# VectorE's exp with a shorter polynomial, 440 instead of 381 tiles on VectorE, and a new order of the steps

## The chip, the cores and the metric

The kernel runs on one core of a Trainium2 chip. The time is device microseconds of one execution, the median of three runs. A profile is one execution seen by the hardware profiler; its span is the time from its first to its last instruction.

## The reference

Four layers, one after the other, each of the form x + attention(layernorm(x)). The weights alternate: layers 1 and 3 use set A, layers 2 and 4 set B. x is 2048 x 512 in float32. There are 32 query heads of 16 dimensions, and one key head and one value head that all of them share.

```python
def _A_ref(x, wq, wk, wv, wo):
    ...
    q = (lambda x, *d: x.transpose(*d))((x @ wq).reshape(B, S, H, Dh), 0, 2, 1, 3)
    k = x @ wk
    v = x @ wv
    scores = jnp.einsum("bhqd,bkd->bhqk", q, k) * (Dh ** -0.5)
    p = _softmax(scores, axis=-1)
    o = jnp.einsum("bhqk,bkd->bhqd", p, v)
    return (lambda x, *d: x.transpose(*d))(o, 0, 2, 1, 3).reshape(B, S, H * Dh) @ wo
...
x = x + _A_ref(_layernorm(x, axis=-1), A_wq, A_wk, A_wv, A_wo)
x = x + _B_ref(_layernorm(x, axis=-1), B_wq, B_wk, B_wv, B_wo)
```

So per layer there are 32 x 2048 x 2048 exponentials, 537 million in all; they are most of the work outside the matmuls.

## The kernel before

**Tiles.** A layer's queries are cut into 4 blocks of 512 rows and 4 groups of 8 heads, and the keys into 32 pieces of 64; each such piece has two tiles of scores, 4096 over the four layers, each of 128 partitions x 1024 float32. The keys stand on the partitions, so the exponentials can be multiplied with V at once, and a column of ones in V gives the softmax's denominators.

**TensorE.** The array is used as eight small arrays of 64 rows x 32 columns: four on its upper 64 rows and four on its lower 64. The two halves of its rows are called row groups 0 and 1 here. A tile of scores (`st`, f16) is eight matmuls of 512 columns, four in each row group. The product with V (`acc`, float32) takes the upper 64 partitions of the exponentials in row group 0 (into `acc0`, letter E) and the lower 64 in row group 1 (into `acc1`, letter O). A float32 matmul stands twice in the trace, once for each of its two passes. E and O each treat 512 columns, either as two steps of 256 columns or, where the order gives E (or O) in two TensorE steps one after the other with nothing between, joined as one step of 512. All other matrix products (queries, keys and values, the output projection) go into one bank named `beside`, also cut into half steps, M or N, of one row group.

**The exponentials.** Most tiles go to ScalarE: `score()` makes the eight matmuls into one of two `st` buffers and one ACTIVATE (L777) into one of 16 buffers `pt`. The others go to VectorE. `score_v()` computes half a tile (letters V, W; 512 columns) into the single bank `by_v`. `exp_first()` (L809, letter I in the order) reads this half out of `by_v`, scales it and converts it to the integer whose bits are nearly the exponential's. When both halves are there, a chain of six instructions over 1024 columns follows (letters 0 and 1, since two chains can be under way): take the mantissa (L823), keep the exponent (L825), three steps of a polynomial in the mantissa (L826, L827, L828), and the product of both (L820).

**The order.** Everything above is written in an order fixed by hand in the string `ORDER`; the engines then run their own queues in that order and wait for each other by semaphores. S is a score for ScalarE; a to s are TensorE steps for the two row groups:

```python
STEPS = {"S": "SS", "a": "EO", "b": "NO", "c": "EN", "d": "MO", "e": "EM", "f": "VO", "g": "EV",
         "h": "WO", "i": "EW", "j": "VM", "k": "MV", "l": "E-", "m": "-O", "n": "N-", "o": "-N",
         "p": "M-", "q": "-M", "r": "V-", "s": "-V"}
```

A dash means that this row group gets nothing in the step. F and P are matmuls over the full 128 rows. X is one VectorE instruction of the layer's other work, G moves `acc` out (L925, L927), D a step of the division, Q a load of queries by a DMA on the SP queue. Y is `touch()` (L906): VectorE copies one column of `beside` into `seen`. It stands where the other row group is to go on in that bank, since the copy waits for TensorE's earlier work on it. All matmuls of the steps are issued in one function, `both()` (L495), row group 0 ahead of row group 1.

Of the kernel before, what the change touches and what calls it, by code (L numbers as in the profile page):

```python
# [49 lines left out]
LEAD = 1013283008.0  # L50
C0, C1, C2, C3 = 37.67991256713867, 23.053848266601562, 12.310662269592285, -0.15703019499778748
# [17 lines left out]
    "bSbISb0b0Sa0sSaaYISa0Sfc1Sc0qSaa1Sc0SccISa0qSaaXSa0SaaXSa0kSbIpSb0hSbIpS0a0Sa0aSiqISa0aSi1qSa0Saa1S0bSaY"
    "aISq0cSc0jSaaISc0SaaXSa0SaaXSr0mISQa0SF0SaaXSXaSPPPSPPGPSGsPISaXX0SaaS1a0Saa1Sa0SaaXSa0aSaXSaaXSa0SaPXSf"  # L70
    "aISl0SaaXSP0PSasXSaaISaXSa0aSXrPSaIaXSPSaaSXsXSaIa0SP0PPSa1Sa0rSaa1S0PPPSa1SPPP0SaaISa0SgaISPP0PSaXSa0aS"
    "hpISb0b0Sa0SgaISc0qSic1Sa0Saa1Sb0pSbpISaaY0SjcISc0qSQaaXSa0Shb1Sb0bSaISlGl0SpbGSb0mSaY0SicISc0qSfa1Sc0Sa"
    "aISc0c0SaSaXaSXXaDSaXXaDSaXXSaDXaXSa0sSaIaSXD0mSaaX1Sf0SaaISXaXSF00SaSaXaDSaXSgXmISaD0SflDSFD0SaaXS0SSIa"
    "XSaXaXD0SF0SXaS0aaSXsaISF0SaaXSa0SaaXSa0ShbIS0pa0SaDaS0kbSbIpSDb0rSalYDSc0SQaa1Sc0SaaISa0a0ScScGqqGSqq0S"
    "aaXSaXSaDXa0SaSaX0aSFXSsDaXISaXa0SXa0SaXX0fScIqSc0qScaDS0aSgaISDb0kSbbISbDpS0b0Sa0aSraISc0cSaXSa0aSaXaS0"
    "fScIcS0qc0Sa0sSaaISb0Shb1Sb0pSa1aS0aScIcS0eSaa0SsaISb0bSaXSa0aSaXrSaIa0Sc0Sc0cSm0SgaISb0pShb1Sa0SaaISQc0"
    "qq0ScSa0aSsaISbGpkGSpp0SaaXSa0SaaISaXSaDa0S0jcISc0qScc1Sj0aSa1Sa0aSb1pSaa0SbSbIbD0SkbSIaaY0SiSaXa0SaaISa"
    "XSaDa0SF0SaXa0SjcSIcq0Sic1Sm0Saa1Sb0pSbbISb0ShbISa0SaaY1Sa0Sic1SaXa0SaScIc0SqcSj0cSaaIS0aShb1S0bSaIaS0bb"
    "0SkbISa0SaaYS1Qgq0SeaXSa0SbaISlGpSl0bGSb0ShbISa0pSha1Sa0SaaY1Sc0SaaISc0cSc0SiaSIc0qSaaXSa0ShbISb0pSk0aIS"
    "a0aSa1Si0cScq1Sc0cSc1SaaY0SapSbIb0SaSaXaXXSrDaISaXXaSDaSXXgmDXSXa0SamXS1aXD0SamISa0SaXrSIaaXS0FSaXSa0aSa"  # L80
    "XrSXaDaS0FSXSDXSXXDSF0SISaXa0SaXsSQaIa0Sa0SF1SaXaS0aSaXaS0arSPGPPGSP0PSPPPISa0SaD0aSsaISa0aSaD1Sa0aSa1Sa"
    "0aSa0SfaISP0PSaaDSa0SaaD0SasSaIaDSa0Sg0aISPP0SaaXSaXSa0aSaX0SaaSXa0rSaaISXFS0faISXl0SaX0aSsXSIaaXX0SrSa1"
    "a0SaS1a0SaaIS0SgaISm0Sf1Sa0aSa1Sa0aSlISa0SsaISa0aSr1SQa0aS1Sa0aSGSGlISa0SgaISaD0Saa1Sa0SaaD1Sf0SaaIS0mSa"
    "0SgaISa0SgaDSm0SaaISDm0SaDaS0jcISc0Scc1Sj0qqSaaY1Sb0Sbb1Sbb0SbSaIaXSa0SicISc0Sic1Sa0qSaIaS0qa0SjaSIaq0Sa"
    "aS1a0ShbS1bp0SbbISb0SaaXSa0sSccISc0Sia1Sa0aScISa0a0SjcSaImY0SQhSa1a0Saa1SbGpSpGppS0pbSaIa0SbSaXaDS0scScI"
    "cS0cSi1cSD0aqSaIaY0Sa0ShbSIb0pSgbDSb0SbaXSaXXaDSaXXSaDaXXSa0SalISaXXSa0aXS0fISaX0aSa1Sa0rSaaXSXl0SFSXa0S"
    "aaISaXaSXa0Sa0Sas0SaaISF0SrSX0SISaXaSXaX0Sa0a0SasSaIa0SFS1aXSa0aSaXSa0aSF0SQaXa0SaSaXa0SajSGqqqGScIc0SaS"
    "a0mSkbISaDa0Sh0SaIa0SkaSIaaD0Skp1Sb0aSl1Sa0aScqISaDa0SjSaYIaSDn0SfaDS0lSa1aS0pSaaISaXsXSaISaXa0SXF0SaaXS"
    "0rSaaXS0aSaX0SaaISaX0SaXXs0SaIa0SSa1a0SrSa1a0SS1aaS0SISa0aSa0sSaaISa0SfaISl0Sa0a0SsSIaa0SQaS1ar0Saa1SGSG"
    "l0SaSaIa0SmSDa0aSsaISa0SaaD1Sr0SaaIS0sSaIa0SS1aaDSr0SaaD0SaSaDS0aaSI0Sa0aSsaISa0Saa1Sr0Saa1S0SaIaS0sSaIa"  # L90
    "S0rSa1aS0aSa1S0aaSIS0agSIm0Saa1Sa0SarS1aa0SSIaa0SsISa0aSr1Sa0aSa1Sa0SaaIS0sSaIaS0QrSa1aS0aSa1SGGSl0lSaIS"
    "a0mSaD0SamS0asSaIaD0SaSfaIS0ls0SaIaS0Sa1aSDa0SarSDa0aSDSa0aSppIpSb0b0SkbSIap0SpaS1ar0Saa1Sc0SccISc0qSiaI"
# [24 lines left out]
    "0a0gSmISa0eSrmXSaXa0SFSaX0SaaISaXS0agXSImXS0aaX0SaSaX0rSaaXXS0Sa1a0SSIa0Sa0SgaISa0Sar1Sa0aSm1Sa0aSISa0aS"
    "Qa0gSmISa0aSrGSGSl0aSaIS0amDS0a0SgaISa0SgaD1Sm0Saa1S0mSaaIS0SafDSaISDa0rSaaDS0cSc1cS0mqScIa0Sm0SgaISb0pS"
# [1239 lines left out]
```

## Time and profile before

| what | value |
|---|---|
| runs | 3474.99, 3476.02, 3476.25 us; median 3476.02 |
| profiled execution, span | 3474.3 us |
| what the median of the runs has above that span | 1.7 us |
| TensorE (PE) busy | 3387.5 us, 98% |
| VectorE (DVE) busy | 3305.2 us, 95% |
| ScalarE (ACT) busy | 3433.9 us, 99% |
| tiles of exponentials on ScalarE, on VectorE | 3715, 381 |
| one-column copies (L906) | 105 |
| granted TensorE clock | 0.97 in the first 100 us, 1.00 after |

The profiled execution's own time is not listed apart; its span is 0.7 us below the lowest of the runs. Busy time is the time in which at least one instruction of the engine is under way. Instructions of one engine overlap at their ends: a group's mean duration is longer than the distance from one start to the next. So a busy share of 98% does not say that the engine could take no more; the distance between starts does.

### The profile page before, as it was taken

The page shows a single profiled execution, that of the slowest core. Times are in us where ns is not written, and L with a number is a line of the kernel's source. Part 1 is how long each engine was busy: PE and PEld are TensorE (multiplying, and loading weights), DVE is VectorE, ACT ScalarE, POOL GpSimd, SP SyncE. Part 2 cuts the span into 40 slices and gives each one's busy share as a digit, 9 for nine tenths or more (in the row PEclk, how much of TensorE's full clock was granted, in tenths as well). Part 3 has the DMA queues.
Part 4 walks back from the last instruction along what each step waited for, and adds up shares of the span by engine and source line. Part 5 has one row for each costly group of instructions (what it writes and reads, how often), then busy time and mean ns, then how long its engine had stood idle before and what let it go on. Part 6 is the DMA issues. An engine that isn't in the chain of part 4 may idle for free.

```text
span 3474.3 us, 202688 instructions
## 1 busy us (share of the span) xinstructions
PE 3387.5 (98%) x96011; PEld 2024.7 (58%) x96011; DVE 3305.2 (95%) x4431; ACT 3433.9 (99%) x3745; POOL 167.8 (5%) x137
## 2 busy tenths in 40 slices
PE   9999999999999999999999999999999999999998
PEld 5566566564556656656455665665546666564554
DVE  4889999999989999999998999999999899999997
ACT  8999999999999999999999999999999999999998
POOL 2001000000000000000000100000000000000000
PEclk9999999999999999999999999999999999999999
DMA  3221111110012111111001211111101121110010
GB/s 102 66 78 39 45 45 36 42 39 25 28 45 69 32 44 47 44 28 46 18 30 54 58 42 34 50 36 34 47 14 44 48 54 37 47 44 25 27 37 21
DMA packets 93811, 147.56 MB, mean 42 GB/s; under 512 B 30056, under 2 KB 47976, under 8 KB 92968
## 3 DMA queue, kind: packets, MB, share of 16 engines
q1 hardware_dynamic: 91400, 133.64, 13.0%
q8 instruction: 752, 12.32, 1.5%
q10 hardware_dynamic: 1568, 0.85, 0.1%
q14 instruction: 91, 0.75, 0.1%
HBM read 90.57 MB, written 34.59 MB: 36 GB/s over the span
## 4 chain that ended last, share of the span: by engine, by line
ACT 44%; PE 42%; DVE 10%; issue 2%; DMA 1%; SPq 0%; POOL 0%; DVEq 0%; ACTq 0%; POOLq 0%
ACT pt L777 44%; PE acc L495 22%; PE st L495 11%; PE beside L495 7%; DVE pt L809 2%; DVE poly L828 1%; PE by_v L495 1%; DVE pt L820 1%; DVE poly L826 1%; DVE poly L827 1%; DVE mant L823 1%; DVE pt L825 1%; PE beside L532 1%; DMA qt<-qs 0%; PE beside L389 0%
## 5 line engine op out<-in xcount | busy, mean ns | idle before, releaser
L777 ACT ACTIVATE pt<-st 128x1024 f32<-128x1024 f32 x3715 | 3419.7, 1078 | 12.7 <-PE st L495 10.7
L495 PE MATMUL acc<-pt,vop 64*32 64x256 f32 (+1 forms) x50536 | 2797.5, 440 | 2.9 <-DVE sum L925 1.2
L495 PE MATMUL st<-qt,kop 64*32 64x512 f16 x29720 | 1685.6, 380 | 68.5 <-ACT pt L777 52.4
L495 PEld LDWEIGHTS <-kop 64*32 64x32 f16 x32768 | 795.6, 90 | 1009.1 <-issue 744.1
L495 PEld LDWEIGHTS acc<-pt,vop 64*32 64x32 f32 x50536 | 1227.6, 106 | 259.0 <-issue 8.1
L809 DVE TENSOR_SCALAR pt<-by_v 128x512 int32<-128x512 f32 x762 | 521.2, 684 | 44.4 <-PE by_v L495 30.8
L828 DVE SCALAR_TENSOR_TENSOR poly<-poly,mant 128x1024 f32<-128x1024 f32 x381 | 467.4, 1227 | 0.7
L820 DVE SCALAR_TENSOR_TENSOR pt<-poly,pt 128x1024 f32<-128x1024 f32 x381 | 466.7, 1225 | 0.6
L827 DVE SCALAR_TENSOR_TENSOR poly<-poly,mant 128x1024 f32<-128x1024 f32 x381 | 464.1, 1218 | 1.8
L826 DVE SCALAR_TENSOR_TENSOR poly<-mant 128x1024 f32<-128x1024 f32 x381 | 464.0, 1218 | 0.0
L495 PE MATMUL beside<-wo,ot 64*32 64x512 f16 x5472 | 402.3, 376 | 0.1
L495 PE MATMUL beside<-xnT,wq 64*32 64x512 f16 x5376 | 390.5, 376 | 0.9 <-DVE gv L432 0.7
L495 PE MATMUL by_v<-qt,kop 64*32 64x512 f16 x3048 | 303.8, 377 | 3.0 <-DMA qt<-qs 1.8
L825 DVE TENSOR_SCALAR pt<-pt 128x1024 int32<-128x1024 int32 x381 | 262.0, 688 | 2.7
L823 DVE TENSOR_SCALAR mant<-pt 128x1024 int32<-128x1024 int32 x381 | 261.3, 686 | 1.8
L495 PEld LDWEIGHTS <-ot 64*32 64x32 f16 x5472 | 165.1, 92 | 43.9 <-issue 4.3
L495 PEld LDWEIGHTS <-wq 64*32 64x32 f16 x5376 | 158.0, 92 | 47.5 <-issue 5.5
L440 POOL TENSOR_TENSOR sq<-qs 128x512 bf16<-128x512 f16 x64 | 100.9, 1576 | 934.4 <-DVE qs L437 934.4
L925 DVE COPY sum<-acc 128x512 f32<-128x512 f32 x126 | 82.5, 682 | 14.4 <-PE acc L495 11.7
L376 POOL TENSOR_TENSOR rstd<-var,nhalf 128x4 f32<-128x4 f32 x15 | 28.8, 1918 | 1235.5 <-DVE var L375 1235.5
L495 PE MATMUL beside<-xnT,wkv 64*32 64x512 f16 x1152 | 84.0, 376 | 0.0
L437 DVE TENSOR_SCALAR qs<-beside 128x512 f16<-128x512 f32 x62 | 42.4, 683 | 18.1 <-PE beside L495 7.3
(125 smaller groups left out, 869.7 us busy)
## 6 DMA issues: line engine op xcount, KB each, us to landing
qt<-qs SPq DMA_DIRECT2D x85, 512.0 KB
qs<-qs SPq DMA_DIRECT2D x127, 128.0 KB
rec<-rs SPq DMA_DIRECT2D x63, 256.0 KB
xs<-xt SPq DMA_DIRECT2D x48, 256.0 KB
xt<-xs SPq DMA_DIRECT2D x48, 256.0 KB
sum<-sum SPq DMA_DIRECT2D x252, 32.0 KB
xt<-in_A_x_dram SPq DMA_DIRECT2D x30, 256.0 KB
out_dram<-xt SPq DMA_DIRECT2D x15, 256.0 KB
```

Of the source, the lines that this page charges most:

```text
L437: V.tensor_scalar(qs[:, 0], ps, BIG, -BIG, ALU.min, ALU.max)
L440: G.tensor_tensor(sq, qs[:, 0], qs[:, 0], ALU.mult)
L495: PE.matmul(o[32 * j:32 * j + 32], w[j][h], x[j][h], start=start, stop=stop, skip_group_check=True, tile_position=(64 * r, 32 * j))
L777: e = A.activation(pts[:, i], st[s], AF.Exp, scale=SCALE / UP / UP).ins
L809: w = V.tensor_scalar(e[:, 512 * r:512 * r + 512], by_v, SCALE / UP / UP * LOG2E * 2.0 ** 23, LEAD, ALU.mult, ALU.add).ins
L820: writer[i] = V.scalar_tensor_tensor(p, poly, C0, p, ALU.add, ALU.mult).ins
L823: lambda: V.tensor_scalar(mant.bitcast(I32), e, 0x7FFFFF, 0x3F800000, ALU.bitwise_and, ALU.bitwise_or),
L825: lambda: V.tensor_scalar(e, e, 0x7F800000, None, ALU.bitwise_and),
L826: lambda: V.scalar_tensor_tensor(poly, mant, C3, mant, ALU.add, ALU.mult),
L827: lambda: V.scalar_tensor_tensor(poly, poly, C2, mant, ALU.add, ALU.mult),
L828: lambda: V.scalar_tensor_tensor(poly, poly, C1, mant, ALU.add, ALU.mult),
L925: V.tensor_copy(sums[pr, odd], acc[odd])
```

## The change

VectorE's polynomial loses one degree and one instruction. The number is now split at the half octave: the mantissa's highest bit goes with the exponent, so the polynomial runs over half the interval, and the exponent's part gets a constant (`HALVES`) put in by the same instruction. The string `ORDER` is a new one: 3656 tiles on ScalarE and 440 on VectorE, 62 letters Y instead of 105, and other letters for the same work: 1322 steps a (EO) instead of 3279, 4724 steps l and m (E or O alone) instead of 210, 1931 steps p and q (M alone) instead of 506, 84 P instead of 144. The functions that read the string are the same.

```diff
-LEAD = 1013283008.0
-C0, C1, C2, C3 = 37.67991256713867, 23.053848266601562, 12.310662269592285, -0.15703019499778748
+LEAD = 1030161728.0
+C0, C1, C2 = 7.247527122497559, 6.331161975860596, 0.5959731936454773
+HALVES = 0x1A827A
 LOG2E = 1.4426950408889634
...
 ORDER = (
...
-    "Sa0aSa0SaaS0aSa0aSaSaaSaSaSaaSSaaSSaaSSaaaa"
+    "S0lSS0S0a0aS0aaSIlmS0lmgSmIaS0alSm0S0aa0SaS0lmSa0aSSaaSaaaa"
 )
...
         chains.append(deque([
-            lambda: V.tensor_scalar(mant.bitcast(I32), e, 0x7FFFFF, 0x3F800000, ALU.bitwise_and,
+            lambda: V.tensor_scalar(mant.bitcast(I32), e, 0x3FFFFF, 0x3F800000, ALU.bitwise_and,
                                     ALU.bitwise_or),
-            lambda: V.tensor_scalar(e, e, 0x7F800000, None, ALU.bitwise_and),
-            lambda: V.scalar_tensor_tensor(poly, mant, C3, mant, ALU.add, ALU.mult),
-            lambda: V.scalar_tensor_tensor(poly, poly, C2, mant, ALU.add, ALU.mult),
+            lambda: V.tensor_scalar(e, e, 0x7FC00000, HALVES, ALU.bitwise_and, ALU.bitwise_or),
+            lambda: V.scalar_tensor_tensor(poly, mant, C2, mant, ALU.add, ALU.mult),
             lambda: V.scalar_tensor_tensor(poly, poly, C1, mant, ALU.add, ALU.mult),
             last]))
```

The longer string moves all lines below it by 36: TensorE's L495 is L531 after the change, ScalarE's L777 is L813, VectorE's L809 is L845, and the chain's lines are L859, L861, L862, L863 and L856.

**First place: VectorE, in the second layer.** These rows are VectorE's queue before, with the chain of one tile (`mant_38546`, `poly_38547`) and the end of the one ahead of it.

```order
L823 TENSOR_SCALAR mant_38546<-pt 128x1024
L828 SCALAR_TENSOR_TENSOR poly_38302<-poly_38302,mant_38301 128x1024
L825 TENSOR_SCALAR pt<-pt 128x1024
L820 SCALAR_TENSOR_TENSOR pt<-poly_38302,pt 128x1024
L809 TENSOR_SCALAR pt<-by_v 128x512
L906 COPY seen<-beside 128x1
L826 SCALAR_TENSOR_TENSOR poly_38547<-mant_38546 128x1024
L827 SCALAR_TENSOR_TENSOR poly_38547<-poly_38547,mant_38546 128x1024
L973 TENSOR_TENSOR sum_38364<-sum_38364,rec 128x512
L828 SCALAR_TENSOR_TENSOR poly_38547<-poly_38547,mant_38546 128x1024
L809 TENSOR_SCALAR pt<-by_v 128x512
L820 SCALAR_TENSOR_TENSOR pt<-poly_38547,pt 128x1024
```

The same engine after, at about the same number of instructions from its start.

```order
L859 TENSOR_SCALAR mant_38967<-pt 128x1024
L861 TENSOR_SCALAR pt<-pt 128x1024
L862 SCALAR_TENSOR_TENSOR poly_38968<-mant_38967 128x1024
L863 SCALAR_TENSOR_TENSOR poly_38968<-poly_38968,mant_38967 128x1024
L856 SCALAR_TENSOR_TENSOR pt<-poly_38968,pt 128x1024
L1008 TENSOR_TENSOR sum_38716<-sum_38716,rec 128x512
L941 COPY seen<-beside 128x1
L845 TENSOR_SCALAR pt<-by_v 128x512 x2
```

The chain has five instructions instead of six; one of the kind 128x1024 with two tensor inputs is gone.

**Second place: TensorE between two tiles of scores.** Before, the commonest interval is E and O in step, either joined (as here, in the first layer) or 256 columns at a time. The rows show the last score of one tile, the product with V, and the first score of the next; `acc0` is row group 0, `acc1` row group 1.

```order
L495 LDWEIGHTS kop0_0_97
L495 MATMUL st1_466<-qt_9757,kop0_0_97 32x512
L495 MATMUL acc0_469<-pt_85,vop0_3_108 32x512 x4
L495 MATMUL acc1_470<-pt_85,vop0_3_108 32x512 x4
L495 LDWEIGHTS kop0_0_97
L495 MATMUL st0_465<-qt_9757,kop0_0_97 32x512
```

After, an interval as it stands 129 times in the program, against 4 times before (this one in the second layer).

```order
L531 LDWEIGHTS kop1_0_101
L531 MATMUL st1_466<-qt_35004,kop1_0_101 32x512
L531 MATMUL acc0_469<-pt_85,vop1_0_109 32x256 x4
L531 MATMUL acc1_470<-pt_85,vop1_0_109 32x256 x4
L531 MATMUL acc0_469<-pt_85,vop1_0_109 32x256 x4
L531 LDWEIGHTS kop1_0_101
L531 MATMUL st0_465<-qt_35004,kop1_0_101 32x512
```

Row group 0 gets twice as many columns here as row group 1; the next interval makes up for it. In numbers of instructions, the product with V has 7500 of 512 columns and 17768 of 256 before, 6724 and 19320 after.

More of the change, by code (lines that the diff above doesn't have):

```diff
@@ new lines @@
+    "QXPPPPPPPPPPSPPXSSXPSPPSPPPSrmSPPPSIPPPSXsaSIlmXlSm0lS0FSXaXaSXaXaXS0lmSQlmXaS0lmSaXXaSlXmX0SlmSGsSGllXm"
+    "ISFXSXrmlSImaXlSXF0SXaS0aXaSXXF0SlmSQXaaXSlm0SFXSalXmSlm0pSrmbISpGppsSInmd0rSpmIlSpmGpsS0maIlS0aSqlq1qlq"
+    "S0qcSc1eSQ1qaeSXmlSXmalXSXFXSlmXlmXXXSXfXlSGmmSXGllSXmaXXSlmXlXSmaXSX1alSm0aSlmXSQXFISaXlmXSlmXSF0SmaXlX"
+    "SaSXXFGSXmllGSslmXSIF0SaXSaXa0Spmp0pSbd0SnmpSQd0dpSalYSolqqSqlqeSqloSilIqSmlXmSXarGSFImlXSml0SllGSXmXalX"
+    "SXm0aSXXlXXmlSXmXlmS0alSQmXaXSl0mSaXXlmSGmS0malSGsSXXaIaSrmISaXa0SFXSXaSXmaXS0FXSmaXlSmlXXSQ0FSlmXlmXSlm"
@@ new lines @@
+    "0SFSXaaXSsqGqS0qclSqIlqqSGlqqqrSYlmId0pSpml0Smp0ppmSppm0pSddpS0aaSQlmYeSXmlSXmalXSXFXSlmXaXXXSXgGpSGpmdI"
+    "pSppmrYSqIcl0qSql0mSql0qeSqlm0SqalS0malSolSQmYppmpSppmdSXalXSmlmpSppmSsYGclIqSoqGrSIem0rSqlq0qSqe0lmSlmI"
+    "Slm0aSpm0ppSpsmppISb0dSQlXmlS0maXSa0lqSql0qqSqlqlq0SqrmlSmGqqSIclSYmpppsSpGppImS0ppmpS0pmd0pSalS0mlmSQlX"
+    "mlSXma0SqelqSoeSqlqqlqSrYmpSpmppIpsSIbm0prSd0bSGlS0lmaSGpmSIma0lSslmSIe0mlSQqlmXSa0aSXlm0SF0SlmlXXmS0iqS"
+    "elIoS0qclSoqGSqrXaXSlXmIaSGlSXbb0S0pmppSQXpmXlmS0pmlSpmXdlXSmXlSalmSrdSXImaXlSXaS0lmcSGqloSGoqS0qelsSYIm"
@@ new lines @@
+    "ap0Sb0pSmp0pdSQpml0SddpSDDa0aSdlSYqqlmlXSslXmSeIeqSqrlqSqqlqqI0Sqa0lGSmqSDlmlqGSlSDDlma0SppmpSQ0dppmSpm0"
+    "ppSddpXSlmlXSmaDDpSgYqqSqlqIrqSqIcl0Smr0lmSl0mSpmpIlmSGpslSGbdISa0aSslm1lSQ0qqlSqql0mlSImaS0alSDpmpmDpSD"
+    "pdrSDDmlImlXSslS1maXlGSFXSaSGbd0SalS1ma0Sqelq0SqqlqSqeDlqDqSDcSIlma0SaS0bbSpmDDrpSIdd0pSgXmlSXmlS0qa0lqS"
+    "qqlq0SqlmlSIqlqqS0lmaSYrpImpSpm0ppsSbIml0Spm0pSmal0SdlSd0aSrmlISpm0lsSm0al0SaSlqIme0SqlmSXalSXma0pSpdpSD"
+    "mppDpmSDrmlISmg0lSqIqcS0c0eSrqqlqISql0mSfa1Sa0lSpmlm0Sp0mlSbImpSQa0lSml0sSqlmlSXmlImSgXlm0SqcISl0qqlq0So"
@@ new lines @@
+    "eSGmfS0alSIpmppSGpn1mS0pmprSma0l0SpmlSmIlpm0SpmlSm0apSsaIlSm0lsSlImql0Sqql0mSalXSmlXmrSIlmS0rFSXmaSDDp0d"
+    "lSpm0lmSIpmlXSpmbSalSXXm0lmS0qelqS0qqlqSc0lqSscSIlmXlmS0rmlISpm0dpS0lmkSdIlS0mllsSm1aS0lmlSm0aSIa0lSrqml"
+    "ISmg0Salm1Slm0SlmaIS0arS0mlmSlImlS0faS0aaSQlImS0asl0SmlImSg1lmGSmSGllS0maS1lm0lSmaSXalSm0aSlmXSIalm0SrmS"
+    "ImaXlSmlS0rmlSXmaS0lSIlmmXSlsSIlmXmlSXrmlSmlXSlmmSlSXXmal0S1PPS0PP0SPPP0SPPS0PPSPS0aXa0SppmpSpmIdp0Sppsp"
+    "mSIppmpS0salS0ma0Sc0eSoeISc0lqSqqreISmlXrmS1cl1qSql1mSqlml0SqlmS0aeSqIemS0lmlsSImlS0ppmg0SpmIbS0pbSpm0pm"
```

289 lines of the change are left out of this document (152 added, 137 removed).

## The prediction

> **What bounds the kernel now.** I read the page's busy line first, then the groups of instructions with shapes kept apart, then the chain that ended last, stages, waits, and at two places the timeline.
>
> ```profile
> PE 3387.5 (98%) x96011; PEld 2024.7 (58%) x96011; DVE 3305.2 (95%) x4431; ACT 3433.9 (99%) x3745; POOL 167.8 (5%) x137
> ACT 44%; PE 42%; DVE 10%; issue 2%; DMA 1%; SPq 0%; POOL 0%; DVEq 0%; ACTq 0%; POOLq 0%
> L777 ACT ACTIVATE pt<-st 128x1024 f32<-128x1024 f32 x3715 | 3419.7, 1078 | 12.7 <-PE st L495 10.7
> 39.48 83.26 ACT pt L777 x91
> 1541.77 32.85 ACT pt L777 x36
> ```
>
> Three engines are busy over 95%, so shares decide nothing; the distance between starts does. The last two rows are pieces of the chain: start, length, engine, count. Undisturbed, ScalarE takes 83.26/91 = 0.915 us a tile, or 32.85/36 = 0.9125; say 0.9135. Over the whole run it takes 3419.7/3715 = 0.9205. So ScalarE sets the time, 3715 x 0.9135 = 3394 us of it, and some 26 us more are waits hidden in overlapping instructions. The wait for scores written openly (10.7) is only a part of them.
>
> ```profile
> 400.00:800.00 400.00, 393.91 (x11601) 242.56 (x11591) 395.89 (x535) 399.81 (x435) 15.79 (x9) 1.00 0.14 41
> 1600.00:2000.00 400.00, 389.42 (x10837) 227.76 (x10829) 383.84 (x508) 396.53 (x431) 17.84 (x11) 1.00 0.14 41
> 2800.00:3200.00 400.00, 390.08 (x11183) 231.46 (x11166) 395.36 (x506) 399.94 (x437) 13.26 (x8) 1.00 0.14 39
> PE st L495 <- ACT pt L777: 52.4, 144, 0.5
> DVE pt L809 <- PE by_v L495: 30.8, 50, 3.0
> ACT pt L777 <- PE st L495: 10.7, 10, 3.3
> ```
>
> The stages (stretch, its length, then busy time and count for PE, PEld, DVE, ACT, POOL, then clock and DMA) say the same throughout: 431 to 437 ACTIVATEs in 400 us, 0.928 to 0.915 us each. TensorE waits for ScalarE (52.4) more than the other way.
>
> How much TensorE has to spare is seen in the timeline.
>
> ```profile
> 1500.73 1.07 PE L495 MATMUL acc<-pt,vop 64*32 64x512 f32 x16
> 1501.59 0.43 PE L495 MATMUL st<-qt,kop 64*32 64x512 f16 x8
> ...
> 1502.67 1.07 PE L495 MATMUL acc<-pt,vop 64*32 64x256 f32 x24
> ...
> 1503.54 0.42 PE L495 MATMUL st<-qt,kop 64*32 64x512 f16 x8
> ```
>
> I call a round the time in which all eight small arrays stream 512 columns once. A joined product with V has two float32 passes of 512 columns, each as long as two rounds; with its 4 rounds it takes 1501.59 - 1500.73 = 0.86 us to the next score, so a round is 0.215 us. By the order, TensorE's steps between the first and the last score sum to 14,190 rounds in each row group, before and after alike within 0.1%. That is 3051 us of ScalarE's 3420: a reserve of a tenth, if both row groups always have work.
>
> **The change part by part.** ScalarE loses 59 of 3715 tiles: 59 x 0.9205 = 54.3 us less, all on the path that sets the end.
>
> VectorE:
>
> ```profile
> L809 DVE TENSOR_SCALAR pt<-by_v 128x512 int32<-128x512 f32 x762 | 521.2, 684 | 44.4 <-PE by_v L495 30.8 <-PE st L495 9.5 <-PE beside L495 1.1
> L828 DVE SCALAR_TENSOR_TENSOR poly<-poly,mant 128x1024 f32<-128x1024 f32 x381 | 467.4, 1227 | 0.7
> L820 DVE SCALAR_TENSOR_TENSOR pt<-poly,pt 128x1024 f32<-128x1024 f32 x381 | 466.7, 1225 | 0.6
> L827 DVE SCALAR_TENSOR_TENSOR poly<-poly,mant 128x1024 f32<-128x1024 f32 x381 | 464.1, 1218 | 1.8
> L826 DVE SCALAR_TENSOR_TENSOR poly<-mant 128x1024 f32<-128x1024 f32 x381 | 464.0, 1218 | 0.0
> L825 DVE TENSOR_SCALAR pt<-pt 128x1024 int32<-128x1024 int32 x381 | 262.0, 688 | 2.7
> L823 DVE TENSOR_SCALAR mant<-pt 128x1024 int32<-128x1024 int32 x381 | 261.3, 686 | 1.8
> L906 DVE COPY seen<-beside 128x1 f32<-128x1 f32 x105 | 15.8, 150 | 11.9 <-PE st L495 6.3 <-PE beside L495 5.4
> ```
>
> The lost polynomial step is 464.1 us. A tile now costs 1.227 + 1.225 + 1.218 + 0.688 + 0.686 + 2 x 0.684 = 6.412 us; 59 more are 378.3. The second operation that the exponent's mask gets is free: L823 has two and takes 686 ns, L825 one and 688. 43 fewer copies are 6.5. So VectorE goes from 3305.2 to 3213 us busy (the number of its instructions falls by 11, so the overlaps stay). In a span near 3436 that is 93.5% against 95.1%: it gets 59 tiles more and still some air. No term of the sum; its cover is that ScalarE sets the time.
>
> The copies' waits were 11.9 us for 105; 43 fewer save some 5 on VectorE, nothing on ScalarE.
>
> Un-joining: 776 fewer products of 512 columns, 1552 more of 256. In the timeline above a stretch with 24 records, in part 256 wide, takes 1503.54 - 1502.67 = 0.87 us, like the joined one. So 0. The other end comes from these rows:
>
> ```profile
> L495 PE MATMUL acc<-pt,vop 64*32 64x256 f32 x35536 | 1923.1, 377 | 2.5 <-DVE sum L925 1.2 <-DVE pt L820 0.5 <-issue 0.5
> L495 PE MATMUL acc<-pt,vop 64*32 64x512 f32 x15000 | 1357.4, 589 | 0.4 <-issue 0.2 <-DVE pt L820 0.2
> L495 PE MATMUL by_v<-qt,kop 64*32 64x512 f16 x3048 | 303.8, 377 | 3.0 <-DMA qt<-qs 1.8 <-DVE pt L809 0.5
> ```
>
> If nothing streamed behind anything, two short ones would cost 2 x 377 - 589 = 165 ns more than a long one: 776 x 2 passes x 0.165/8 = 32 us on TensorE, which its reserve holds.
>
> The unevenness is the term that I had to choose. Between two scores the busier row group has, summed over all intervals, 14,869 rounds before and 15,682 after: 813 more, 175 us. But summed over pairs of intervals it is 14,824 and 14,797: what one interval gives to one row group, the next gives to the other. If a row group may run ahead over a score, the unevenness costs nothing; if it may not, up to 175 us. The trace shows which. At 1644 us the program has three products for row group 0 (twelve `beside`), then the eight scores:
>
> ```profile
> 1644.52 0.61 PE L495 MATMUL beside<-xnT,wkv 64*32 64x512 f16 x8
> 1644.91 0.40 PE L495 MATMUL st<-qt,kop 64*32 64x512 f16 x4
> 1644.95 0.40 PE L495 MATMUL beside<-xnT,wkv 64*32 64x512 f16 x4
> 1645.14 0.39 PE L495 MATMUL acc<-pt,vop 64*32 64x256 f32 x4
> 1645.16 0.40 PE L495 MATMUL st<-qt,kop 64*32 64x512 f16 x4
> ```
>
> Four of the scores start at 1644.91, ahead of the third product at 1644.95 which stands before them in the program, and the other four 0.25 us later. So a row group does overtake the other, by at least a round. The Trainium skill, page "TensorE: Matmul & The Clock Gate", section "The mechanism", says otherwise: matmuls start and end strictly in program order, and only weight loads are pulled ahead. This trace disagrees, by the 0.25 us; by the page the sum would be the first rival's.
>
> What leaks through all the same? If all 26 us of hidden waits came from today's unevenness (14,869 - 14,190 = 679 rounds, 146 us), the share would be 0.18, and the new 175 us would give 31 us of waits. If none, 0. I take the middle, +16, since TensorE waits for ScalarE more often than the reverse.
>
> Queues: SP issues the same transfers, the 84 loads of queries among them; one of these has held TensorE up for 1.8 us in sum (the `by_v` row), taken as 0, at most a few us where a load now stands later. POOL has the same work and is 5% busy. What lies ahead of the first tile and behind the last is not touched.
>
> Sum against the profiled execution: 3474.3 - 54.3 + 16 = 3436. The median of the runs lies 1.7 above that span: 3438. The ends of the mechanism itself: all tiles at the pace of the best stage, 3656 x 0.9153 = 3346, is 73 less (3402); at the pace of the worst, 0.9281, 3393, is 27 less (3449); waits of 31 give 3453.
>
> **Rivals.**
>
> 1. *Strict order of the row groups.* A waiting row group holds up the other, and the 813 rounds count. For each pair of intervals I take the larger of ScalarE's 2 x 0.915 us and TensorE's rounds at 0.215, and add them up: before 3472 either way, after 3421 if the lead is carried, 3540 if not. (These sums lie 50 us above ScalarE's real 3420, since a pair can lean on the next; only their differences count.) So the time would be 3476 + 68 = 3544. Against it speak the rows at 1644.91. It decides from 31% of the 175 us on, since 54 are gained. 8%.
>
> 2. *The half tiles in `by_v` become the brake.* That bank is single; a half is written only when VectorE has read the last one, and everything behind it in TensorE's queue, scores for ScalarE too, waits along. There are 118 more such halves, of 0.684 us reading each. Today TensorE lost 0.5 us to this (`by_v` row), while VectorE waited 30.8 us for TensorE, so the bank is mostly ahead. If each new half cost half of its reading time, 40 us come back: 3476 - 54 + 16 + 40 = 3478, no change. If each cost the whole, 3519. From 54 us on (0.46 us a half) the change loses. 8%: half of that within the bound of no change, half slower or slightly faster.
>
> 3. *The tiles taken from ScalarE don't shorten it*, since its pace is set by scores arriving at what TensorE can do: 3474 to 3478. Against it: 0.915 us in the best stage with no less work (11183 matmuls) than in the worst (10837). 4%.
>
> 4. *More than the sum*: the new order also removes today's waits; all tiles at 0.9153 or better, under 3408. 4%.
>
> **How the numbers follow.** My forecast, 3438, has 76%. Its own range is 3402 to 3453 by the bounds above, some us wider for a late load: up to 3458. To leave out no more than 2 in 10 the range cuts the best end to 3408 and takes in rival 2's lower part, to 3466. A difference under 0.2% (7 us) can't be told from none. Faster: 76 + 4 + 2 = 82%, and 1 of rival 3's, so 83; same: rival 3's other 3 and 4 of rival 2: 7; slower: 8 of rival 1 and 2 of rival 2: 10.
>
> **What the profile after would show.** Right: 3656 ACTIVATEs at 0.92 to 0.925 us in the group's row; three groups of 128x1024 with two tensor inputs on VectorE at 440 each and 1.22 us; VectorE busy near 3213; `seen` 62 times; in the timeline, scores in two groups of four far oftener, with other products between. Wrong: ScalarE's row at 0.95 us a tile or TensorE named often as what ends its waits (rival 1); idle time of TensorE ahead of `by_v` released by VectorE's L845, tens of us (rival 2); the polynomial's steps longer than 1.25 us, which nothing here suggests.

## The result, and the profile after

| what | before | after |
|---|---|---|
| median of the runs | 3475.68 us (4 runs, 3474.99 to 3476.25) | 3445.33 us (4 runs, 3444.14 to 3446.91) |
| profiled execution, span | 3474.3 us | 3445.1 us |
| that execution's own time | not listed | 3446.91 us |

The ratio after to before is 0.9913, 95% interval 0.9899 to 0.9927: 30 us or 0.87% faster, well above the 7 us that can be told from no change. 3438 was predicted, with a range of 3408 to 3466. Repeated later, the changed kernel took 3445.15 us (below, e11). So the direction held and the size nearly: 7 us of the 38 that were promised are missing.

The page's busy line after, the chain by engine, ScalarE's group, and the longest of its pieces in the chain (start, length, engine, count):

```profile
PE 3371.2 (98%) x97983; PEld 2102.8 (61%) x97983; DVE 3267.9 (95%) x4420; ACT 3389.2 (98%) x3686; POOL 133.5 (4%) x137
PE 58%; ACT 28%; DVE 8%; issue 2%; DMA 1%; SPq 0%; DVEq 0%; ACTq 0%
L813 ACT ACTIVATE pt<-st 128x1024 f32<-128x1024 f32 x3656 | 3374.9, 1083 | 28.5 <-PE st L531 23.8 <-PE beside L531 0.2 <-PE acc L531 0.2
1650.23 22.68 ACT pt L813 x25
```

ScalarE's group fell from 3419.7 to 3374.9 us of busy time (44.8 less), and the idle time ahead of it rose from 12.7 to 28.5 (15.8 more). The difference, 29.0, is the whole gain: the spans differ by 29.2. Its undisturbed pace has not suffered, 22.68/25 = 0.907 us a tile. The mean over the run is 3374.9/3656 = 0.9231 (0.92 to 0.925 was predicted; 0.9205 before). In the chain, TensorE and ScalarE have changed places: 58% and 28% now, where they had 42% and 44% before.

The three stretches and the waits, in the same columns as before:

```profile
400.00:800.00 400.00, 394.36 (x11553) 248.44 (x11541) 387.23 (x530) 397.95 (x433) 12.09 (x10) 1.00 0.14 40
1600.00:2000.00 400.00, 392.31 (x11674) 247.84 (x11665) 378.92 (x518) 396.13 (x430) 17.80 (x14) 1.00 0.15 43
2800.00:3200.00 400.00, 391.14 (x11423) 239.16 (x11416) 388.49 (x496) 398.24 (x433) 6.49 (x5) 1.00 0.13 38
...
DVE pt L845 <- PE by_v L531: 40.1, 70, 3.0
PE st L531 <- ACT pt L813: 28.9, 84, 0.5
ACT pt L813 <- PE st L531: 23.8, 42, 5.6
DVE seen L941 <- PE beside L531: 20.0, 25, 3.2
```

ScalarE does 430 to 433 tiles in 400 us; before it was 431 to 437. So the loss is in no one of these stages alone. ScalarE now waits openly for scores 23.8 us in 42 places (10.7 in 10 before), and TensorE waits for ScalarE 28.9 us in 84 places (52.4 in 144 before): the balance has tipped.

VectorE's groups, and the half tiles on TensorE:

```profile
L845 DVE TENSOR_SCALAR pt<-by_v 128x512 int32<-128x512 f32 x880 | 601.8, 684 | 54.7 <-PE by_v L531 40.1 <-PE st L531 9.7
L863 DVE SCALAR_TENSOR_TENSOR poly<-poly,mant 128x1024 f32<-128x1024 f32 x440 | 538.7, 1225 | 3.8
L862 DVE SCALAR_TENSOR_TENSOR poly<-mant 128x1024 f32<-128x1024 f32 x440 | 537.4, 1222 | 0.0
L856 DVE SCALAR_TENSOR_TENSOR pt<-poly,pt 128x1024 f32<-128x1024 f32 x440 | 537.3, 1222 | 4.0
L861 DVE TENSOR_SCALAR pt<-pt 128x1024 int32<-128x1024 int32 x440 | 303.6, 690 | 3.7
L859 DVE TENSOR_SCALAR mant<-pt 128x1024 int32<-128x1024 int32 x440 | 302.1, 687 | 13.6
L941 DVE COPY seen<-beside 128x1 f32<-128x1 f32 x62 | 9.3, 150 | 22.7 <-PE beside L531 20.0 <-PE st L531 2.0
...
L531 PE MATMUL by_v<-qt,kop 64*32 64x512 f16 x3520 | 352.3, 378 | 7.9 <-DVE pt L845 4.6 <-DMA qt<-qs 1.8 <-DVE den L989 0.5
```

Three groups of 440 with two tensor inputs at 1.222 to 1.225 us, and 62 copies, as predicted. The mask with two operations (L861) costs 690 ns instead of 688. TensorE lost 4.6 us to the bank `by_v`.

The scores in the timeline of TensorE, at the same distance from the start as the rows shown of before:

```profile
1645.21 0.79 PE L531 MATMUL acc<-pt,vop 64*32 64x256 f32 x12
1645.74 0.40 PE L531 MATMUL st<-qt,kop 64*32 64x512 f16 x4
1645.82 0.54 PE L531 MATMUL acc<-pt,vop 64*32 64x256 f32 x8
1646.03 0.40 PE L531 MATMUL st<-qt,kop 64*32 64x512 f16 x4
```

One row group has started its four scores 0.29 us ahead of the other, whose products stand between. Counted over all tiles by the starts in the trace, the second four scores start 100 ns or more behind the first four in 660 of 3715 tiles before and in 1297 of 3656 after.

### The profile page after: what moved, and what is told of

It reads as the page before. It is cut to its first block, busy times and chain, and to the rows that moved or that the text cites. A ratio compares the mean times of both kernels' runs of the same rounds, so it can differ in the third digit from the quotient of the medians.

```text
span 3445.1 us, 206723 instructions
## 1 busy us (share of the span) xinstructions
PE 3371.2 (98%) x97983; PEld 2102.8 (61%) x97983; DVE 3267.9 (95%) x4420; ACT 3389.2 (98%) x3686; POOL 133.5 (4%) x137
## 4 chain that ended last, share of the span: by engine, by line
PE 58%; ACT 28%; DVE 8%; issue 2%; DMA 1%; SPq 0%; DVEq 0%; ACTq 0%
PE acc L531 31%; ACT pt L813 28%; PE st L531 15%; PE beside L531 9%; PE by_v L531 2%; DVE pt L845 1%; DVE poly L862 1%; DVE poly L863 1%; PE beside L425 1%; DVE pt L856 1%; DVE mant L859 1%; PE beside L568 1%; DMA qt<-qs 1%; DVE pt L861 1%; DMA rec<-rs 0%
## 5 line engine op out<-in xcount | busy, mean ns | idle before, releaser
L813 ACT ACTIVATE pt<-st 128x1024 f32<-128x1024 f32 x3656 | 3374.9, 1083 | 28.5 <-PE st L531 23.8
L531 PE MATMUL acc<-pt,vop 64*32 64x256 f32 (+1 forms) x52088 | 2904.6, 432 | 5.3 <-issue 2.0
L531 PE MATMUL st<-qt,kop 64*32 64x512 f16 x29248 | 1784.8, 380 | 44.4 <-ACT pt L813 28.9
L531 PEld LDWEIGHTS acc<-pt,vop 64*32 64x32 f32 x52088 | 1341.9, 106 | 273.5 <-DVE sum L960 15.0
L531 PEld LDWEIGHTS <-kop 64*32 64x32 f16 x32768 | 799.2, 90 | 904.4 <-issue 620.0
L845 DVE TENSOR_SCALAR pt<-by_v 128x512 int32<-128x512 f32 x880 | 601.8, 684 | 54.7 <-PE by_v L531 40.1
L863 DVE SCALAR_TENSOR_TENSOR poly<-poly,mant 128x1024 f32<-128x1024 f32 x440 | 538.7, 1225 | 3.8
L856 DVE SCALAR_TENSOR_TENSOR pt<-poly,pt 128x1024 f32<-128x1024 f32 x440 | 537.3, 1222 | 4.0
L862 DVE SCALAR_TENSOR_TENSOR poly<-mant 128x1024 f32<-128x1024 f32 x440 | 537.4, 1222 | 0.0
L531 PE MATMUL beside<-xnT,wq 64*32 64x512 f16 x5760 | 432.0, 376 | 1.0 <-DVE qs L480 0.4
L531 PE MATMUL beside<-wo,ot 64*32 64x512 f16 x5376 | 390.4, 376 | 1.2 <-DVE xt L500 1.1
L531 PE MATMUL by_v<-qt,kop 64*32 64x512 f16 x3520 | 352.3, 378 | 7.9 <-DVE pt L845 4.6
L859 DVE TENSOR_SCALAR mant<-pt 128x1024 int32<-128x1024 int32 x440 | 302.1, 687 | 13.6
L861 DVE TENSOR_SCALAR pt<-pt 128x1024 int32<-128x1024 int32 x440 | 303.6, 690 | 3.7
L531 PEld LDWEIGHTS <-wq 64*32 64x32 f16 x5760 | 167.7, 92 | 46.6 <-issue 10.5
L531 PEld LDWEIGHTS <-ot 64*32 64x32 f16 x5376 | 153.9, 92 | 40.7 <-issue 5.2
L531 PE MATMUL beside<-xnT,wkv 64*32 64x512 f16 x1344 | 97.1, 376 | 1.2 <-issue 1.2
L500 DVE SCALAR_TENSOR_TENSOR xt<-beside,xt 128x512 f32<-128x512 f32 x61 | 42.0, 688 | 6.1 <-PE beside L531 4.0
```

What stands on the lines that cost most here:

```text
L500: V.scalar_tensor_tensor(x, ps, 1 / VS / WS, x, ALU.mult, ALU.add)
L531: PE.matmul(o[32 * j:32 * j + 32], w[j][h], x[j][h], start=start, stop=stop, skip_group_check=True, tile_position=(64 * r, 32 * j))
L813: e = A.activation(pts[:, i], st[s], AF.Exp, scale=SCALE / UP / UP).ins
L845: w = V.tensor_scalar(e[:, 512 * r:512 * r + 512], by_v, SCALE / UP / UP * LOG2E * 2.0 ** 23, LEAD, ALU.mult, ALU.add).ins
L856: writer[i] = V.scalar_tensor_tensor(p, poly, C0, p, ALU.add, ALU.mult).ins
L859: lambda: V.tensor_scalar(mant.bitcast(I32), e, 0x3FFFFF, 0x3F800000, ALU.bitwise_and, ALU.bitwise_or),
```

## The experiments

Two theories stood at the start. Mine: ScalarE's count of tiles sets the time, VectorE's shorter chain is only what pays for the 59 tiles, a row group that runs ahead over a score hides most of the unevenness, and what leaks through is a little of it. The rivals: the shorter chain brings the time by itself; un-joining the products takes away the missing 7 us; TensorE's load as a whole has become the bound; the row groups don't run ahead.

**e1, the shorter chain alone.** The kernel before, old order, 381 tiles.

```diff
-            lambda: V.scalar_tensor_tensor(poly, mant, C3, mant, ALU.add, ALU.mult),
-            lambda: V.scalar_tensor_tensor(poly, poly, C2, mant, ALU.add, ALU.mult),
+            lambda: V.scalar_tensor_tensor(poly, mant, C2, mant, ALU.add, ALU.mult),
+            lambda: None,
```

(with the new masks and constants).

> The kernel before, old order and 381 tiles, with the new five-step chain (the letter of the step that fell away does nothing); 381 x 1.218 = 464 us of VectorE's instructions go. Theory (ScalarE sets the pace, VectorE's time is covered): 3464 to 3477 us, at most 0.3% faster, since 3715 tiles stay on ScalarE; VectorE busy near 2870. Rival (VectorE's chain is late for TensorE, and the shorter chain alone brings the gain): 3440 to 3455.

Measured: 3471.41 us, ratio 0.9987 (0.9978 to 0.9996), some 4 us less. Its busy line and its chain:

```profile
PE 3382.5 (97%) x96011; PEld 2019.1 (58%) x96011; DVE 2921.6 (84%) x4050; ACT 3431.4 (99%) x3745; POOL 152.6 (4%) x137
ACT 55%; PE 39%; DVE 3%; issue 2%; DMA 1%; SPq 0%; DVEq 0%; ACTq 0%
```

VectorE lost 383.6 us of busy time and the kernel about 4: it was not the bound at 95%. So the rest of the 30 us, some 26, comes with the moved tiles and the order that moves them. No run moves the tiles without the order's other changes, so these two are not told apart. VectorE's busy time was expected near 2870 and came out at 2921.6; the account of the prediction below comes back to it.

**e2, the new order without the shorter chain.** The first polynomial step is done twice, so VectorE has six instructions a tile again.

```diff
-            lambda: V.scalar_tensor_tensor(poly, mant, C2, mant, ALU.add, ALU.mult),
+            lambda: [V.scalar_tensor_tensor(poly, mant, C2, mant, ALU.add, ALU.mult) for _ in range(2)],
```

> The changed kernel with one polynomial step of each tile done twice (same result), so a chain as long as before on 440 tiles: 440 x 1.222 = 538 us more for VectorE. Theory (the shorter chain is what makes room for 440 tiles in this order): VectorE has 177 us idle in a span of 3445, so it becomes the limit: 3750 to 3850 us. Rival (VectorE's idle time and overlaps take it in, and the order alone brings the gain): 3445 to 3500.

Measured: 3945.25 us, ratio 1.1353 (1.1332 to 1.1373). The busy line, the chain, and the groups of the half tiles and of ScalarE:

```profile
PE 3486.7 (88%) x97983; PEld 2093.0 (53%) x97983; DVE 3788.3 (96%) x4860; ACT 3463.8 (88%) x3686; POOL 133.7 (3%) x137
DVE 80%; PE 10%; issue 6%; ACT 2%; DMA 1%; SPq 0%; DVEq 0%; POOL 0%; POOLq 0%
L531 PE MATMUL by_v<-qt,kop 64*32 64x512 f16 x3520 | 354.6, 383 | 272.0 <-DVE pt L845 268.8 <-DMA qt<-qs 0.8
L813 ACT ACTIVATE pt<-st 128x1024 f32<-128x1024 f32 x3656 | 3449.5, 1043 | 452.4 <-PE st L531 417.7 <-PE by_v L531 8.5 <-PE acc L531 3.9
```

This is what my second rival looks like when it happens: TensorE idle for 268.8 us ahead of `by_v`, ScalarE for 417.7 us behind TensorE. The shorter chain is the condition of the 440 tiles. One VectorE instruction of 1.22 us more in each tile, 539 us in sum, cost 500 us, nearly all of it and some 100 more than I had expected: TensorE is dragged along in `by_v`. VectorE's share reads 96% here and 95% in the changed kernel: the share does not tell the two apart, the wait ahead of `by_v` does.

**e3, no joined products.** E and O always go in steps of 256 columns; 6724 joined products fall.

```diff
-                    carry[r] = parts[r][0][2] == 0 and STEPS.get(then, "SS")[r] == w
+                    carry[r] = False
```

> The changed kernel with no product with V joined: 6724 matmuls of 512 columns become 13448 of 256, eight times the un-joining of the change. Theory (un-joining is free, since the next round streams behind the last): 3438 to 3453 us. Rival (each un-joined one costs TensorE 2 x 165 ns / 8 = 41 ns, so 277 us here, over the reserve): 3500 us or more, and the 776 of the change would explain most of the 25 us that the change lost.

Measured: 3508.79 us, ratio 1.0099 (1.0084 to 1.0115), 63.5 us above the changed kernel. ScalarE's group:

```profile
L813 ACT ACTIVATE pt<-st 128x1024 f32<-128x1024 f32 x3656 | 3395.3, 1074 | 67.1 <-PE st L531 54.9 <-PE by_v L531 2.3 <-PE beside L531 0.4
```

So un-joining is not free; the prediction had taken it as 0, and my expectation failed. The time is over the rival's 3500. Yet un-joining does not cost what the single records would say either, 6724 x 2 x 0.165/8 = 277 us. It is 63.5/6724 = 9.4 ns for each product on the path; the change's 776 would be 7 us at that price.

**e4, less work on TensorE.** The two small terms of each projection run over 64 of 512 columns; the rest of them is left out.

```diff
+            k = 512 if n % 3 == 0 else 64
-            return "beside", beside, cols(w), [x] * 4, first, last
+            return "beside", beside[:, :k], cols(w), [x[:, :k]] * 4, first, last
```

> The changed kernel with the two small terms of every projection (high by low, low by high) multiplied for 64 of 512 columns only; the rest of these terms is left out. TensorE has 954 rounds = 205 us less per row group. Theory (what is lost in ScalarE's waits comes from how the two row groups' work lies in the intervals with products with V, not from TensorE's total): 3425 to 3442 us, 5 to 20 faster than the changed kernel. Rival (TensorE's total load makes ScalarE wait): all of 3374.9 - 3656 x 0.9135 = 35 us hidden and 24 us open waiting goes: 3386 to 3400.

Measured: 3439.57 us, ratio 0.9896 (0.9881 to 0.9911), 5.8 us below the changed kernel. That interval overlaps the changed kernel's, so the size is loose. But the rival's 3386 to 3400 is far away: 205 us less work in each row group does not bring the 45 to 59 us that it forecast, so TensorE's load as a whole is not what holds the changed kernel up.

```profile
ACT 46%; PE 37%; DVE 12%; issue 3%; DMA 1%; SPq 1%; DVEq 0%; ACTq 0%
```

The chain's shares swing back to ScalarE (46% against 28%) for 5.8 us: with two engines this close, a share of the chain says which of them is a hair later, not what a relief is worth.

**e8, the same on the kernel before.**

> The kernel before, with the two small terms of each projection over 64 of 512 columns only (those columns' rest is left out): the counterpart of the run on the changed kernel, which gained 5.8 us. Theory (TensorE's whole load bounds neither kernel; what leaks through is single uneven intervals, which are fewer here): a gain of 2 to 8 us, 3467 to 3474. Rival (the old order was held up by TensorE's load more than the new one, which is where the new one's gain comes from): a gain of 15 us or more, 3460 or less.

Measured: 3471.55 us, ratio 0.9988 (0.9978 to 0.9997), 4.9 us less. So the projections weigh on the old order about as much as on the new one, and the theory's range held.

**e5 and e6, no running ahead.** Four one-column matmuls over all 128 rows stand ahead of each tile's scores, in the old and in the new order. Neither row group can pass them alone: in both traces there is no tile whose second four scores start 100 ns or more behind the first four.

```diff
+        for j in range(4):
+            PE.matmul(st[s][32 * j:32 * j + 32, 0:1], bones[:, 0], bones[:, 0, 0:1], start=True, stop=True,
+                      skip_group_check=True, tile_position=(0, 32 * j))
         both([[(("st", s, r), st[s][:, 512 * r:512 * r + 512]) + moving(n, r)] for r in range(2)])
```

> The kernel before, with four one-column matmuls over all 128 rows ahead of each tile of scores, into the bank the scores are about to fill: neither row group can start its scores before the other has finished what stands ahead of them. Theory (the row groups of the old order are nearly even between two scores, 679 rounds or 146 us over all intervals, and part of it lies where ScalarE is waited for anyway): a small loss, 20 to 110 us, so 3495 to 3585. Rival (the row groups wait for each other at every score already, so the lead does not matter): only the small matmuls' own time, the same in both orders, difference to the next run under 30 us. The two runs are read together: theory, the changed order loses 100 to 200 us more than this one.

> The changed kernel with the same four small matmuls ahead of each tile of scores. Theory (the new order lives on one row group running ahead over a score; the busier row group has 15,682 rounds against 14,190 in all, 1492 rounds or 321 us over all intervals, of which some lie where ScalarE is waited for anyway): a loss of 150 to 300 us against the changed kernel, so 3595 to 3745, and 100 to 200 us more than the old order loses. Rival (the row groups wait for each other at every score already): the same loss as in the old order within 30 us, and still some 30 us below that run.

Measured: 4169.28 us in the old order (ratio 1.1993, 1.1973 to 1.2013) and 4304.86 in the new one (1.2384, 1.2364 to 1.2405). That is 693 and 860 us more than without. The size of each was missed by far: the small matmuls themselves are dear, as their groups show (old order, then new), with ScalarE's group of the new order behind them.

```profile
L773 PE MATMUL st<-bones 128*32 128x1 bf16 x14860 | 698.2, 177 | 22.5 <-ACT pt L780 17.4 <-DVE gv L432 0.7
...
L809 PE MATMUL st<-bones 128*32 128x1 bf16 x14624 | 687.0, 177 | 8.2 <-ACT pt L816 5.3
L816 ACT ACTIVATE pt<-st 128x1024 f32<-128x1024 f32 x3656 | 3660.4, 1025 | 602.5 <-PE st L531 541.7 <-DVE pt L859 0.3 <-DVE mant L862 0.3
```

That cost is nearly common to both (59 tiles fewer make it 11 us less in the new order). What is left between them is what the runs were for: 859.5 - 692.9 = 166.7 us. The prediction's account, 813 rounds more in the busier row group, 175 us, is the most that an order would lose that can't run ahead. But the 166.7 also hold the 30 us that the new order gains without the barrier. With it TensorE is 95 and 97% of the chain, so the 59 tiles taken from ScalarE can hardly count, and the two runs as they stand are 135.6 us apart. The price measured is thus 136 to 167 us, some of it other than unevenness (un-joining, 7 us by e3). In the timeline of the new order with the barrier, all eight scores start together:

```profile
1644.38 0.19 PE L809 MATMUL st<-bones 128*32 128x1 bf16 x4
1644.50 0.41 PE L531 MATMUL st<-qt,kop 64*32 64x512 f16 x8
1644.73 0.39 PE L531 MATMUL beside<-xnT,wq 64*32 64x512 f16 x4
1644.74 0.39 PE L531 MATMUL acc<-pt,vop 64*32 64x256 f32 x4
```

So the unevenness is real, its price is near the one worked out, and the changed kernel escapes most of it because a row group runs ahead over a score: with the barrier the new order is slower than the old one, without it 30 us faster. That is as near as the runs come to the first rival.

**e9 and e10, a faster ScalarE in both orders.** The exponentials of 960 of 1024 columns only; those of the other 64 are left out, on ScalarE and in VectorE's chain, and all matmuls stay.

```diff
-        e = A.activation(pts[:, i], st[s], AF.Exp, scale=SCALE / UP / UP).ins
+        e = A.activation(pts[:, i, 0:960], st[s][:, 0:960], AF.Exp, scale=SCALE / UP / UP).ins
...
+        p, e, mant, poly = (t[:, 0:960] for t in (p, e, mant, poly))
```

> The changed kernel with the exponentials of 960 of 1024 columns only, on ScalarE (the ACTIVATE) and in VectorE's chain; the other 64 columns' exponentials are left out, all matmuls stay. Per column ScalarE takes at most 0.9135/1024 = 0.89 ns, so a tile gets up to 57 ns shorter, 3656 x 0.057 = 208 us. Theory (ScalarE still sets the time; TensorE has by pairs of intervals 14,797 rounds or 3181 us, with some 70 us at the ends 3250): 3250 to 3340. Rival (the changed order has made TensorE the bound, as its 58% of the chain would say): under 45 us gained, 3400 or more.

> The kernel before with the same edit, 960 of 1024 columns: 3715 x 0.057 = 212 us at most. Theory (ScalarE sets the time in both, and the old order's single intervals are more even): 3255 to 3340, and at least as fast as the changed kernel with this edit, since the 59 tiles matter less once TensorE is near. Rival (the old order has the smaller reserve): 3350 or more.

Measured: 3353.21 us in the new order (ratio 0.9648, 0.9633 to 0.9663) and 3380.23 in the old one (0.9730, 0.9715 to 0.9745). Against their own kernels on the same chip (3445.15, 3475.17) that is 91.9 and 94.9 us. The chain and ScalarE's longest undisturbed piece, first of the new order, then of the old (two pieces):

```profile
PE 73%; DVE 11%; ACT 11%; issue 2%; DMA 1%; SPq 1%; DVEq 0%; ACTq 0%
1672.68 12.97 ACT pt L814 x15
```

```profile
PE 76%; DVE 10%; ACT 10%; issue 2%; DMA 1%; SPq 1%; POOL 0%; DVEq 0%
1497.03 13.06 ACT pt L778 x15
...
3116.47 12.74 ACT pt L778 x15
```

Undisturbed, a tile takes 12.74/15 = 0.849 to 13.06/15 = 0.871 us, so it became 0.043 to 0.064 us shorter. Over 3656 tiles 157 to 235 us were offered, and 92 came through: 39 to 59%. In the old order 159 to 239 were offered and 95 came, 40 to 60%. The distances between ScalarE's starts over the whole traces narrow this down. Without those that are plainly waits (over 0.93 us, or 0.885 in the narrower runs) their mean is 0.910 us in the full kernels and 0.863 in the narrower ones; that offers 171 us in the new order and 175 in the old one, and 54% came through in both. My theory failed in both orders, and so did the new order's rival: that run stands between the two. The old order's rival (3350 or more) has its number, though the smaller reserve that it argued from does not show, since both orders pass on the same part. The old order, which I held to be at least as fast, is 27 us slower, about the old distance. Two things follow. First, ScalarE does not set the time alone in either order: of a relief this size about half is lost to the other engines. Second, the two orders lose alike, which speaks against the new one being nearer to TensorE's limit. The edit shortens VectorE's chain too (3155 instead of 3268 us busy in the new order), so these runs are not of ScalarE alone.

**e7, e11 and e12, more joins.** The changed kernel, in which E or O is joined also where only steps of the other row group stand before its next one: 656 more joined products. e11 is the changed kernel again, on e12's chip.

```diff
-                    carry[r] = parts[r][0][2] == 0 and STEPS.get(then, "SS")[r] == w
+                    carry[r] = parts[r][0][2] == 0 and w in [STEPS.get(t, "SS")[r] for t in then]
...
+        def upto(l):
+            return l[:next((n for n, t in enumerate(l) if t in "SFP"), len(l))]
...
-                step(what, on_pe[0] if on_pe else "S")
+                step(what, upto(on_pe))
```

> The changed kernel, order kept, with E or O joined to 512 columns also where the next step of the same row group comes after steps of the other row group alone (not over a score): 656 more joined products. Theory (an un-joined product costs 63.5 us / 6724 = 9.4 ns wherever it stands): 656 x 9.4 = 6 us less, 3437 to 3442. Rival (the price of the un-joined products arises only in intervals in which TensorE is the bound, and the 656 stand in others; or a product that is done earlier makes the row groups less even): no gain, 3443 to 3449, or a loss.

> The changed kernel again, unaltered, on the same chip as the next run, so that the 3.7 us between the two can be judged: 3442 to 3448 by either theory.

> The changed kernel with 656 more joined products, beside the unaltered one on the same chip. Theory (an un-joined product costs on the path 5.7 to 9.4 ns): 3 to 7 us less than the run before it. Rival (the first difference was that of chips or runs): under 1.5 us.

Measured: 3441.61 us (ratio to before 0.9899, 0.9883 to 0.9916); then 3445.15 for the changed kernel (0.9914, 0.9900 to 0.9927) beside 3441.07 with the joins (0.9904, 0.9889 to 0.9919). Twice it is some 4 us less, 5.7 to 6.2 ns for each of the 656. But the intervals overlap, single runs reach from 3440.5 to 3446.9 (9 runs) and from 3438.5 to 3445.9 (8 runs), and the means of these, 3444.7 and 3441.6, are 3 us apart: likely, not shown. It is the fastest version that I ran with all of the work, clearly ahead of the kernel before.

## Why the prediction was right, and where it was off

- *ScalarE's 59 tiles.* Right. Busy time fell by 44.8 us and the whole gain can be read from ScalarE's row. At the undisturbed 0.9135 us the tiles are 53.9 us; the spans gave 29.2, so 24.7 were lost again. That the order's other changes gain nothing of their own is argued, not shown.
- *The unevenness, +16.* The term that was mis-sized, by 9 us: 24.7 leaked, inside its ends of 0 and 31. The +16 was the middle of the two ends, with no row behind it, so that it came as near as this was in part luck. Its mechanism holds as far as e5 and e6 show it: of the 175 us of unevenness worked out, 136 to 167 appear when a row group can't run ahead, and most of it is hidden otherwise. But my reason for what leaks, a share of the new unevenness, isn't shown. The narrower exponentials lost about half of what ScalarE was offered with no change of order, and the moved tiles lost 24.7/53.9 = 46%. That alone could account for all of it. Against this stands that a relief three times as large may lose a larger part than a small one does, which leaves room for unevenness and un-joining. The traces speak against unevenness, too. ScalarE's distances between starts exceed 0.9035 us a tile by 72 us in sum before and by 94 after. Some 17 of the 22 more lie behind pairs of intervals in which neither row group has more than six rounds besides the scores; with the two scores that is 8 x 0.215 = 1.72 us, less than ScalarE's two tiles. There the loss for each tile rose alike behind two even intervals and behind pairs with an uneven one, from 9 or 10 ns to 17 or 18. Earlier unevenness may still be carried into them, so how the 25 us divide stays open.
- *Un-joining at 0.* Too low: e3 prices an un-joined product at 9.4 ns, 7 us for 776; the smaller price from e7 and e12, 5.7 to 6.2 ns or 4 to 5 us, rests on a difference that isn't shown. By itself this would cover most of the 7 us by which the forecast was off. My row was one stretch with 24 records, that is with four products un-joined, 0.01 us longer than the joined one: 2.5 ns each, at the timeline's grain. I took that for none. Where the rest of the price falls, beside the streaming itself, the runs don't show. The other end, 32 us, was too high for the path.
- *TensorE's reserve of a tenth.* The count (14,190 rounds) stands, but as a reserve it was read too generously: with tiles some 5% shorter only half came through in either order, and TensorE took 73 and 76% of the chain. A sum over the run hides the intervals in which TensorE is late: in e9 and e10 some three quarters of what ScalarE's distances have above their commonest, 0.86 us, lie behind the third of the pairs of intervals in which a row group has seven rounds or more besides the scores.
- *VectorE near 3213 us.* Off: 3267.9. The instructions are as costed: the six groups of the chain and the halves sum to 2821 us now and, with the seventh, to 2907 before. Their overlap is what changed. VectorE's busy time is a union, and the chain's instructions stand more often beside a wait instead of a neighbour (54.7 us ahead of L845 against 44.4, 13.6 ahead of L859 against 1.8). e1 shows the same by itself: 464.1 us of instructions were removed and only 383.6 of busy time. "Overlaps stay" was the step that failed. It cost nothing here.
- *The copies.* 43 fewer, but the rest waits longer, 22.7 against 11.9 us; 5 us less were expected. It is VectorE's time and no term of the sum.
- *Strict order, 8%.* The time refutes it, and e6 shows what it would look like. The Trainium skill, page "TensorE: Matmul & The Clock Gate", section "The mechanism", has matmuls start strictly in program order. The trace disagrees for row groups that are used apart: the scores of one tile start 0.29 us apart with the other group's products between, and with the barrier that prevents it the new order is 136 us slower than the old one.
- *`by_v` as the brake, 8%.* Refuted for this kernel (4.6 us), shown as a danger by e2 (268.8 us).
- *The tiles don't shorten ScalarE, 4%*, and *more than the sum, 4%*. Neither came, though the first was nearer to the truth than its chance says: about half of each relief is lost.

## What to carry to other kernels

Cost a tile that leaves the slowest engine by its undisturbed pace, and then ask what part of such a relief the next engine lets through. One run in which that engine does a few per cent less work tells it; here it was about half, in two orders and at one size of relief, while a reserve counted over the whole run promised nearly all. Where instructions on two row groups are uneven, add them up over pairs of intervals and not over single ones, as long as nothing that uses both stands between. And a busy share of 95% can mean room (the changed kernel) or a brake (e2): look for the wait that the engine causes.

## What the runs showed of the hardware that I had not expected

- Four one-column matmuls over all 128 rows ahead of a tile of scores that uses the two row groups apart cost 0.19 us a tile (692.9/3715) in the old order and 0.24 in the new one (859.5/3656): 177 ns is the mean of one in the trace. I read the 0.05 between the orders as mostly the running ahead that they prevent.
- Joining two float32 products of 256 columns into one of 512 is worth 9.4 ns on the path here (e3), perhaps less where fewer are joined, though the single records (377 and 589 ns) would suggest 2 x 165/8 = 41.
- Removing an instruction of 1218 ns from VectorE's chain of 381 tiles took only 383.6/381 = 1.007 us of busy time each.
